# kv with v as loaded as the stationary operand, in four 32-column tiles of TensorE, one head each

## The chip, the cores and the metric

One core of a Trainium2 chip runs the whole program. The metric is the device time of one execution in microseconds (us); lower is better. Engines in the text and in the profile lines: PE is TensorE (its matmuls; PEld is its weight loads), DVE is VectorE, ACT is ScalarE, POOL is GpSimd, SP is SyncE, which issues most DMAs.

## The reference

Two stages, run one after the other: attention with polynomial (sketched) features, then a feed-forward layer (FFN) with squared ReLU.

```python
def phi(x):                                   # r = 8, so 64 features
    a = einsum('rd,bhsd->bhsr', S1, x)
    b = einsum('rd,bhsd->bhsr', S2, x)
    return einsum('bhsi,bhsj->bhsij', a, b).reshape(..., 64)
q_p, k_p = phi(q), phi(k)                     # batch 4, heads 4, seq 1088, head_dim 32
kv  = einsum('bhsf,bhsd->bhfd', k_p, v)
z   = sum(k_p, axis=2)                        # the normaliser
num = einsum('bhsf,bhfd->bhsd', q_p, kv)
den = einsum('bhsf,bhf->bhs', q_p, z)[..., None] + 1e-06
x   = (num / den) as (4352, 128)
out = (relu(x @ w_in) ** 2) @ w_out           # w_in 128x2048, w_out 2048x128
```

## The kernel before

The FFN is a stream of 192 steps (4 batches x 3 chunks of up to 384 rows x 16 column blocks). Each step is one fp16 matmul into `pg`, a ReLU on ACT, a square on ACT or DVE, and one fp32 matmul into `po`. A small planner places the attention of batch n in the steps of the FFN of batch n-1, so that only batch 0's attention stands alone, at the start.

The change touches `kv`. Per batch there are nine row tiles of 128 positions (the last has 64). `kp` holds the 4 x 64 features of a tile. In the kernel before, v is copied into `va`, where each head has 33 columns, 32 of v and one of ones, so that one matmul gives kv and the normaliser. (Of a matmul's two operands, the stationary one is what PEld loads, and the moving one is what the PE record gives as its form, here 128x64.) Rows 64 to 127 of `va`'s last tile are zeroed once, so the short last tile runs on 128 rows too:

```python
# v into va: POOL for batches 1 to 3 (three copies each), ACT and POOL for batch 0
def a_v(b, part, eng, t0=0, n=4):
    ...                                       # [cut] 33 columns per head, column 32 is 1.0

def a_kv(b, t):                               # nine times per batch
    kvp = st[b, "kvp"]
    kp, c0 = st[b, "kp", t]
    for h in range(H):
        c = 64 * (h % 2)                      # two column tiles of 64: heads 0,2 and heads 1,3
        nc.tensor.matmul(
            kvp[c : c + 33, 64 * (h // 2) : 64 * (h // 2) + 64],
            va[b % 2][:, 132 * t + 33 * h : 132 * t + 33 * h + 33],   # stationary, 128 x 33
            kp[:, c0 + 64 * h : c0 + 64 * h + 64],                    # moving, 128 x 64, fp32
            start=(t == 0 and h < 2), stop=(t == NT - 1), skip_group_check=True)

def a_kvz(b):
    kvt = wpool.tile([128, 128], F32, tag="kvt", name="kvt")
    nc.vector.transpose(kvt[:, :], st[b, "kvp"][:, 0:128])
    ...                                       # [cut] eight small copies into the block matrix kvz
    st[b, "kvz"] = kvz                        # read by the nd matmuls: q features x kvz
```

The features of k come from another batch of matmuls (`kf`) which in batches 1 to 3 uses four 32-column tiles already:

```python
for i in range(2):
    for p0 in range(4):
        nc.tensor.matmul(kf[32 * p0 : 32 * p0 + 32, ...], sk[:, 32 * i : 32 * i + 32], kq[...])
```

Of the kernel before, what the change touches and what calls it, by code (L numbers as in the profile page):

```python
# [9 lines left out]
F32 = mybir.dt.float32  # L10
# [3 lines left out]
def _ap(t: bass.AP, p0: int, np_: int, off: int, free):  # L14

    p = list(t.ap)[0]
    return bass.AP(
        t.tensor, t.offset + p0 * p[0] + off, [[p[0], np_]] + [list(d) for d in free]
    )
# [33 lines left out]
def kernel(  # L53
# [11 lines left out]
    nc = tc.nc  # L65

    B, H, S, D = 4, 4, 1088, 32
# [8 lines left out]
    NT = (S + 127) // 128  # L76
    SP = 128 * NT
    TW = [min(128, S - 128 * t) for t in range(NT)]
    E = 2
# [6 lines left out]
    add = mybir.AluOpType.add  # L86
    mult = mybir.AluOpType.mult
# [6 lines left out]
    cpool = ctx.enter_context(tc.tile_pool(name="const", bufs=1))  # L94
    bpool = ctx.enter_context(tc.tile_pool(name="perb", bufs=2))
    wpool = ctx.enter_context(tc.tile_pool(name="work", bufs=2))
    fpool = ctx.enter_context(tc.tile_pool(name="ffn", bufs=5))
    psf = ctx.enter_context(tc.tile_pool(name="psf", bufs=2, space=bass.MemoryType.PSUM))
    psa = ctx.enter_context(tc.tile_pool(name="psa", bufs=1, space=bass.MemoryType.PSUM))
# [30 lines left out]
    kn, qn, vn = {}, {}, {}  # L130
# [52 lines left out]
    kq = cpool.tile([128, SP], F32)  # L183
    nc.gpsimd.memset(_ap(kq, 0, 128, 2 * 32 * NT + 256, [[32 * NT, 2], [1, 32]]), 0.0)
    nc.gpsimd.memset(qT[:, S:SP], 0.0)
    va = []
    for i in range(2):
        t_ = cpool.tile([128, NT * 132], F32, tag=f"va{i}", name=f"va{i}")
        nc.gpsimd.memset(t_[:, (NT - 1) * 132 : NT * 132], 0.0)
        nc.gpsimd.memset(_ap(t_, 0, 128, 32, [[33, NT * H]]), 1.0)  # L190
        va.append(t_)
    kvzs = []
    for i in range(2):
        t_ = cpool.tile([128, E * 132], F32, tag=f"kvz{i}", name=f"kvz{i}")
        nc.gpsimd.memset(t_[:], 0.0)
        kvzs.append(t_)

    st = {}

    def a_kv0(b):  # L200

        st[b, "kvp"] = psa.tile([128, 512], F32, tag="acc", bufs=2, name="kvp")
        nc.vector.memset(st[b, "kvp"][:, 0:128], 0.0)

    a_kv0(0)

    def a_kT(b, part):
        if b > 0 and part < 2:
# [35 lines left out]
    mask_b = [8 + l % 8 for l in range(32)]  # L244
    mask_a = [[4 * e + l // 8 for l in range(32)] for e in range(E)]


    def a_v(b, part, eng, t0=0, n=4):
        a = va[b % 2]
        copy = eng.copy if eng is nc.scalar else eng.tensor_copy  # L250
        if part < 2:
            copy(
                _ap(a, 0, 128, 528 * part + 132 * t0, [[33, H], [132, n], [1, 32]]),
                _ap(vn[b], 0, 128, 512 * part + 32 * t0, [[128, H], [32, n], [1, 32]]),
            )
        else:
            copy(
                _ap(a, 0, 64, 8 * 132, [[33, H], [1, 32]]),
                _ap(vn[b], 0, 64, 1024, [[32, H], [1, 32]]),
            )  # L260

    def a_qT(b, c0, c1):
        nc.vector.transpose(qT[:, c0:c1], qn[b][:, c0:c1])  # L263
# [22 lines left out]
    def a_fs(b, g):  # L286

        n = KG[b][g][1]
        kf = st[b, "kf", g]
        fs = wpool.tile([128, 5 * 64], F32, tag="fs", name="fs")  # L290
        if b == 0:
            for i in range(2):
                nc.scalar.copy(  # L293
                    fs[:, 32 * n * i : 32 * n * i + 32 * n],
                    _ap(kf, 0, 128, 32 * i, [[64, n], [1, 32]]),
                )
        else:
            nc.vector.transpose(fs[:, 0 : 64 * n], kf[:, 0 : 64 * n])
        st[b, "fs", g] = fs

    def a_kp(b, g):
        t0, n = KG[b][g]
        fs = st[b, "fs", g]
        kp = wpool.tile([128, 5 * 256], F32, tag="kp", name="kp", bufs=4)
        nc.vector.tensor_tensor(  # L305
            out=_ap(kp, 0, 128, 0, [[64, 4 * n], [8, 8], [1, 8]]),
            in0=_ap(fs, 0, 128, 0, [[8, 4 * n], [1, 8], [0, 8]]),
            in1=_ap(fs, 0, 128, 32 * n, [[8, 4 * n], [0, 8], [1, 8]]),
            op=mult,
        )  # L310
        for i in range(n):
            st[b, "kp", t0 + i] = kp, 256 * i

    def a_kv(b, t):
        kvp = st[b, "kvp"]
        kp, c0 = st[b, "kp", t]

        for h in range(H):
            c = 64 * (h % 2)
            nc.tensor.matmul(  # L320
                kvp[c : c + 33, 64 * (h // 2) : 64 * (h // 2) + 64],
                va[b % 2][:, 132 * t + 33 * h : 132 * t + 33 * h + 33],
                kp[:, c0 + 64 * h : c0 + 64 * h + 64],
                start=(t == 0 and h < 2),
                stop=(t == NT - 1),
                skip_group_check=True,
            )

    def a_kf2(b):
# [3 lines left out]
    def a_kv9(b):  # L333
        for t in range(NT):
            a_kv(b, t)

    def a_kvz(b):
        kvt = wpool.tile([128, 128], F32, tag="kvt", name="kvt")
        nc.vector.transpose(kvt[:, :], st[b, "kvp"][:, 0:128])
        kvz = kvzs[b % 2]  # L340

        def block(eng, h):
            (eng.copy if eng is nc.scalar else eng.tensor_copy)(
                _ap(kvz, 32 * h, 32, 33 * h, [[132, E], [1, 32]]),
                _ap(kvt, 64 * (h % 2), 32, 64 * (h // 2), [[32, E], [1, 32]]),
            )

        def ones(eng, h):
            (eng.copy if eng is nc.scalar else eng.tensor_copy)(  # L349
                _ap(kvz, 32 * h, 32, 33 * h + 32, [[132, E]]),  # L350
                _ap(kvt, 64 * (h % 2) + 32, 32, 64 * (h // 2), [[32, E]]),
            )


        for h in range(H):
            block(nc.vector if b > 0 or h < 2 else nc.scalar, h)
        for h in range(H):
            ones(nc.gpsimd if b > 0 or h > 1 else nc.vector, h)
        st[b, "kvz"] = kvz

    def a_qc(b, ch, pool=psa, tag="feat"):
# [274 lines left out]
    def replicated(j_, c0, c1, pool, tag):  # L636
        rep[j_, c0] = pool.tile([128, 512], F32, tag=tag, name="rep")
        nc.tensor.matmul(
            rep[j_, c0][:, 0 : c1 - c0], sr[:, 128 * j_ : 128 * j_ + 128], qT[:, c0:c1]
        )  # L640

    def products(c0, c1):
        for e in range(E):
            nc.vector.tensor_tensor(
                out=st[0, "qp", 0, e][:, c0:c1], in0=rep[e, c0][:, 0 : c1 - c0],
                in1=qb[:, c0:c1], op=mult,
            )

    qb = wpool.tile([128, 384], F32, tag="qb", name="qb")
    for e in range(E):  # L650
        st[0, "qp", 0, e] = bpool.tile([128, 384], F32, tag="qp", bufs=4, name="qp")
    replicated(2, 0, 128, psf, "pg")
    a_v(0, 0, nc.scalar)
    a_kp(0, 0)
    a_kp(0, 1)
    for t in range(4):
        a_kv(0, t)
    replicated(0, 0, 128, psa, "feat")
    replicated(1, 0, 128, psa, "tr")
    a_fs(0, 2)  # L660
    a_fs(0, 3)
    a_v(0, 2, nc.gpsimd)
    for h in range(H):
        nc.gpsimd.tensor_copy(
            sq[32 * h : 32 * h + 32, 32 * h : 32 * h + 16], s_T[:, 0:16]
# [2 lines left out]
    make_identity(nc, iden[:])  # L668
    iden16 = cpool.tile([128, 128], F16)
    nc.gpsimd.tensor_copy(iden16[:], iden[:])  # L670
    a_v(0, 1, nc.scalar, 0, 2)
    a_kp(0, 2)
    a_v(0, 1, nc.scalar, 2, 2)
    a_kp(0, 3)
    for t in range(4, 9):
        a_kv(0, t)
    nc.scalar.copy(qb[:, 0:128], rep[2, 0][:, 0:128])
    products(0, 128)

    replicated(2, 128, 384, psf, "pg")  # L680
    replicated(0, 128, 384, psf, "po")
    replicated(1, 128, 384, psf, "po")
    a_kvz(0)
    nc.scalar.copy(qb[:, 128:384], rep[2, 128][:, 0:256])
    products(128, 384)
# [24 lines left out]
    P = _Plan(NS + 4, {"PE": 0.95, "DVE": 1.2, "ACT": 0.6, "POOL": 5.0, "SP": 9.0})  # L710
    for m in range(B * 3 - 1):
        b, ch = divmod(m, 3)
        s0 = 16 * (m + 1)
# [45 lines left out]
    for n in range(1, B):  # L759
        s0 = 48 * (n - 1)  # L760
        P.fix(("ld", n), "SP", 0.0, s0, loads, n)
        for part in range(3):
            P.add(("v", n, part), "POOL", 1.0, [], a_v, n, part, nc.gpsimd, first=s0 + 6)
        for part in range(3):
            P.add(("kT", n, part), "DVE", (0.71, 0.71, 0.2)[part], [], a_kT, n, part, first=s0 + 6)

        need = [("kT", n, part) for part in range(3)] + [("qa", n - 1, 2, 1)]
        P.add(("kf", n), "PE", 1.2, need, a_kf2, n)
        for g in range(2):
            P.add(("fs", n, g), "DVE", 0.4, [("kf", n)], a_fs, n, g)  # L770
            P.add(("kp", n, g), "DVE", 1.15 + 0.3 * g, [("fs", n, g)], a_kp, n, g)
        P.add(("qT", n), "DVE", 1.25, [], a_qT, n, 0, S, first=P.at["kT", n, 2] + 1)
        P.add(("kv0", n), "DVE", 0.15, [("kp", n, 0), ("x3", n - 1, 1)], a_kv0, n)
        need = [("kp", n, 0), ("kp", n, 1), ("kv0", n)] + [("v", n, part) for part in range(3)]
        P.add(("kv", n), "PE", 2.2, need, a_kv9, n)
        q_tasks(n, (0,), 0)
        P.add(("kvz", n), "DVE", 0.9, [("kv", n)], a_kvz, n)
        nd_tasks(n, (0,))
        for ch in (1, 2):
            q_tasks(n, (ch,), 0)  # L780
            nd_tasks(n, (ch,))
# [59 lines left out]
```

## Time and profile before

| | before |
|---|---|
| median time | 203.81 us (203.60 to 204.49, 4 runs) |
| span of the profiled execution | 202.5 us |
| PE / DVE / ACT / POOL busy | 96% / 71% / 71% / 29% |
| kv batch on PE, batches 1 to 3, each | 2.23 us |
| first FFN matmul starts at | 17.42 us |

Lines of the page of the kernel before: busy time of each engine, and the chain of work that ended last as shares by engine and by line.

```profile
span 202.5 us, 3743 instructions
## 1 busy us (share of the span) xinstructions
PE 194.5 (96%) x1209; PEld 127.0 (63%) x1209; DVE 143.0 (71%) x388; ACT 144.1 (71%) x325; POOL 58.2 (29%) x249
...
## 4 chain that ended last, share of the span: by engine, by line
PE 87%; DMA 6%; ACT 2%; SPq 1%; issue 1%; DVE 0%; ACTq 0%
```

PE is the bound: 87% of the chain is PE, the other engines almost nothing. So a microsecond taken off PE's stream between the first and the last FFN matmul is worth a microsecond, and one taken off POOL is worth nothing.

The chain in order of time around batch 1's kv, kernel before (columns: start, length, what):

```profile
40.06 0.65 PE po L513 x2
40.71 2.13 PE kvp L320 x72
42.84 0.27 PE pg L490
```

The 36 fp32 matmuls are 72 records, since an fp32 matmul is two passes. The FFN stream stands still for 2.13 us, three times in the program.

The single records of that batch show what sets its length. These are the times from one record's start to the next, in ns, from the trace; the first number is from the `po` record before:

```
before, kv batch of batch 1 (72 records):
416, 7, 74, 7, 49, 6, 50, 6, 49, 7, 49, 7, 49, 7, ... 49, 7, 152
```

Two records on different column tiles start 7 ns apart, and the pair repeats every 56 ns: a *round*. 36 rounds of 56 ns are 2.02 us. A plain `po` record at 384 columns takes 322 ns, so the 416 ns on entering hold 94 ns that are lost when the tiling changes, and leaving costs about as much again (152 ns in place of 49). I count a kv batch from the end of the `po` record before to the start of the next FFN matmul: 2.554 - 0.322 = 2.23 us.

The start of the program, chain of the kernel before:

```profile
8.00 8.13 DMA w_in_100<-in_moe_w_in_dram
16.15 1.04 ACT w_in L687
17.20 0.45 ACT xT L471 x2
17.69 0.28 PE pg L490
```

### The profile page before, as it was taken

How to read it: one execution, taken by the hardware profiler on the slowest of the kernel's cores; microseconds unless marked ns; L12 is line 12 of the kernel's file. 1: busy time of each engine (PE TensorE's matmuls, PEld its weight loads, DVE VectorE, ACT ScalarE, POOL GpSimd, SP SyncE). 2: the span in 40 equal slices, each digit the busy share in tenths (PEclk: the TensorE clock that was granted, in tenths of full speed). 3: DMA queues.
4: the chain of work that ended last, by engine and by line, in shares of the span. 5: the costliest groups of instructions: out<-in, count | busy, mean ns of one | idle time of the engine just before them, and what ended most of it. 6: DMA issues, size and time to landing. Idle time of an engine off the chain costs nothing.

```text
span 202.5 us, 3743 instructions
## 1 busy us (share of the span) xinstructions
PE 194.5 (96%) x1209; PEld 127.0 (63%) x1209; DVE 143.0 (71%) x388; ACT 144.1 (71%) x325; POOL 58.2 (29%) x249
## 2 busy tenths in 40 slices
PE   7997999999999999999999999999999999999990
PEld 2873675577667555667576655768576655556990
DVE  3975976876497677977757788766847767666750
ACT  3637988857796877686887777686888765766740
POOL 4826447010525830012826500011825300000000
PEclk9999999999999999999999999999999999999999
DMA  6699421110011662020105640020102020110201
GB/s 184 198 263 258 129 72 23 19 23 0 19 31 27 183 169 35 3 39 5 37 13 105 176 132 0 3 41 0 39 12 51 0 32 0 19 23 0 39 0 32
DMA packets 31356, 12.32 MB, mean 61 GB/s; under 512 B 23338, under 2 KB 29930, under 8 KB 31338
## 3 DMA queue, kind: packets, MB, share of 16 engines
q1 hardware_dynamic: 30886, 12.00, 24.3%
q8 instruction: 9, 0.15, 0.3%
q10 hardware_dynamic: 452, 0.10, 0.3%
q14 instruction: 9, 0.07, 0.1%
HBM read 8.78 MB, written 2.23 MB: 54 GB/s over the span
## 4 chain that ended last, share of the span: by engine, by line
PE 87%; DMA 6%; ACT 2%; SPq 1%; issue 1%; DVE 0%; ACTq 0%
PE po L513 55%; PE pg L490 15%; PE nd L389 7%; DMA w_in_100<-in_moe_w_in_dram 4%; PE kvp L320 3%; PE qc L363 3%; DMA vn<-in_v_dram 2%; PE pt L530 2%; PE kf L279 2%; ACT gt L499 2%; SPq L104 1%; ACT w_in L687 1%; SPq L114 0%; ACT xT L471 0%; SPq L160 0%
## 5 line engine op out<-in xcount | busy, mean ns | idle before, releaser
L499 ACT ACTIVATE gt<-pg 128x384 f32<-128x384 f32 (+2 forms) x193 | 89.0, 464 | 38.5 <-PE pg L490 37.6
L490 PE MATMUL pg<-xT,w_in 128*128 128x384 f16 (+2 forms) x193 | 61.1, 316 | 1.1 <-ACT xT L471 0.7
L545 POOL COPY br<-beta 32x3 f32<-32x3 f32 x192 | 42.6, 222 | 50.1 <-DVE beta L453 42.5
L490 PEld LDWEIGHTS <-w_in 128*128 128x128 f16 x193 | 18.9, 98 | 19.6 <-issue 1.9
L373 DVE STREAM_SHUFFLE qa<-qc 128x384 f32<-128x384 f32 x22 | 12.0, 592 | 0.1
L389 PEld LDWEIGHTS nd<-kvz_127,qp 128*128 128x128 f32 x72 | 10.0, 190 | 3.0 <-DVE qp L378 0.2
L553 DVE STREAM_TRANSPOSE oT<-po 128x384 f32<-128x384 f32 (+1 forms) x11 | 6.2, 564 | 7.9 <-PE po L513 7.9
L378 DVE TENSOR_TENSOR qp<-qa,qb 128x384 f32<-128x384 f32 x22 | 11.7, 567 | 0.1
L389 PEld LDWEIGHTS nd<-kvz_125,qp 128*128 128x128 f32 x72 | 9.9, 190 | 2.7 <-issue 0.2
L305 DVE TENSOR_TENSOR kp<-fs 128x512 f32<-128x512 f32 (+3 forms) x10 | 10.8, 1108 | 0.5 <-ACT fs L293 0.4
L389 PE MATMUL nd<-kvz_127,qp 128*128 128x132 f32 x72 | 10.3, 277 | 0.0
L389 PE MATMUL nd<-kvz_125,qp 128*128 128x132 f32 x72 | 10.2, 280 | 0.0
L349 POOL COPY kvz_127<-kvt 32x2 f32<-32x2 f32 x8 | 1.5, 185 | 26.3 <-PE pg L490 16.9
L363 PE MATMUL qc<-qT,sq 128*128 128x384 f32 x22 | 8.8, 491 | 0.0
L446 DVE TENSOR_TENSOR xs<-nd,sc 128x384 f16<-128x384 f32 (+2 forms) x13 | 6.7, 522 | 0.3
L263 DVE STREAM_TRANSPOSE qT<-qn 128x1088 f32<-128x1088 f32 (+2 forms) x5 | 5.3, 1061 | 2.3 <-DMA qn<-in_q_dram 2.3
L368 DVE STREAM_SHUFFLE qb<-qc 128x384 f32<-128x384 f32 x11 | 6.5, 588 | 0.0
L559 DVE TENSOR_TENSOR ob<-oT,br 128x384 f32<-128x384 f32 (+1 forms) x11 | 6.3, 572 | 0.0
L405 DVE TENSOR_SCALAR den<-nd 128x12 f32<-128x12 f32 x12 | 2.0, 170 | 5.8 <-PE nd L389 5.8
L410 DVE TENSOR_REDUCE mx<-nd 128x12 f32<-128x384 f32 x12 | 5.9, 495 | 0.0
L363 PEld LDWEIGHTS qc<-qT,sq 128*128 128x128 f32 x22 | 4.1, 190 | 2.7
L621 PE MATMUL warm<-zero 128*128 128x512 f16 x13 | 4.6, 516 | 1.2 <-DVE zero L143 1.2
(711 smaller groups left out, 414.2 us busy)
## 6 DMA issues: line engine op xcount, KB each, us to landing
vn<-in_v_dram SPq DMA_DIRECT2D x32, 64.0 KB, 2.8
kn<-in_k_dram SPq DMA_DIRECT2D x3, 544.0 KB, 8.1
qn<-in_q_dram SPq DMA_DIRECT2D x3, 544.0 KB, 3.5
out_dram<-ob SPq DMA_DIRECT2D x32, 48.0 KB, 1.8
w_in_100<-in_moe_w_in_dram SPq DMA_DIRECT2D x2, 512.0 KB
w_o<-in_moe_w_out_dram SPq DMA_DIRECT2D x2, 512.0 KB, 11.4
out_dram<-ob SPq DMA_DIRECT2D x12, 40.0 KB, 1.8
qn<-in_q_dram SPq DMA_DIRECT2D x1, 352.0 KB
```

Source lines behind the costliest of these rows:

```text
L305: nc.vector.tensor_tensor(out=_ap(kp, 0, 128, 0, [[64, 4 * n], [8, 8], [1, 8]]), in0=_ap(fs, 0, 128, 0, [[8, 4 * n], [1, 8], [0, 8]]), in1 ...
L363: nc.tensor.matmul(qc[:, 0:384], sq[:, :], qT[:, 384 * ch : 384 * ch + 384])
L368: nc.vector.stream_shuffle(in_=st[b, "qc", ch][:, 0:384], out=qb[:, :], mask=mask_b)
L373: nc.vector.stream_shuffle(in_=st[b, "qc", ch][:, 0:384], out=qa[:, :], mask=mask_a[e])
L378: nc.vector.tensor_tensor(out=qp[:, :], in0=st[b, "qa", ch, e][:, :], in1=st[b, "qb", ch][:, :], op=mult)
L389: nc.tensor.matmul(nd[:, 132 * o : 132 * o + 132], st[b, "qp", ch, e][:, 128 * o : 128 * o + 128], st[b, "kvz"][:, 132 * e : 132 * e + 132 ...
L446: nc.vector.tensor_tensor(out=_ap(st[b, "xs", ch], 0, 128, 128 * o, [[32, 4 * n], [1, 32]]), in0=_ap(st[b, "nd", ch], 0, 128, 132 * o, [[3 ...
L490: nc.tensor.matmul(pg[:, c0:c1], w_in[:, 128 * c : 128 * c + 128], st[b, "xT"][:, 384 * ch + c0 : 384 * ch + c1],)
L499: nc.scalar.activation(gt[:, c0:c1], pg[:, c0:c1], Relu)
L513: nc.tensor.matmul(st["po", b, ch][:, c0:c1], w_o[:, 128 * c : 128 * c + 128], g2s[i][1][:, c0:c1], start=first, stop=(c == NFF - 1), skip ...
L545: nc.gpsimd.tensor_copy(_ap(st[b, "br"], 32 * dm, 32, 12 * ch + p0, [[4, 3]]), st[b, "beta"][32 * p0 : 32 * p0 + 32, 3 * ch : 3 * ch + 3],)
L559: nc.vector.tensor_tensor(out=_ap(ob, 0, 128, 0, [[32, n // 32], [1, 32]]), in0=_ap(st["oT", b, ch], 0, 128, 0, [[32, n // 32], [1, 32]]), ...
```

## The change

The intent is to make kv cheaper on PE and to drop the copies of v. v is used as loaded, 32 columns per head, so that four heads fit in four 32-column tiles. The normaliser then needs matmuls of its own, with a stationary of ones. To keep these few, DVE first adds the features of eight tiles into one (batches 1 to 3); in batch 0 this is not done, and it pays 36 extra matmuls. The block matrix is made by one masked product in place of eight copies.

```diff
     def a_kv(b, t):
-        kvp = st[b, "kvp"]
+        if t == 0:
+            st[b, "kvp"] = psa.tile([128, 512], F32, tag="acc", bufs=2, name="kvp")
         kp, c0 = st[b, "kp", t]
+        n, v0, dv = (128, 512 * (t // 4) + 32 * (t % 4), 128) if t < 8 else (64, 1024, 32)
         for h in range(H):
-            c = 64 * (h % 2)
             nc.tensor.matmul(
-                kvp[c : c + 33, 64 * (h // 2) : 64 * (h // 2) + 64],
-                va[b % 2][:, 132 * t + 33 * h : 132 * t + 33 * h + 33],
-                kp[:, c0 + 64 * h : c0 + 64 * h + 64],
-                start=(t == 0 and h < 2),
+                st[b, "kvp"][32 * h : 32 * h + 32, 0:64],
+                _ap(vn[b], 0, n, v0 + dv * h, [[1, 32]]),
+                kp[0:n, c0 + 64 * h : c0 + 64 * h + 64],
+                start=(t == 0),
...
+    def a_z(b, kp, c0, last):                 # four matmuls, stationary ones[128, 32]
...
+    def a_ks1(b):                             # DVE: 128x1024 add; a_ks2: 512, then 256
...
     def a_kv9(b):
         for t in range(NT):
             a_kv(b, t)
+        a_z(b, *st[b, "kp", 8], False)
+        a_z(b, st[b, "ks"], 0, True)
...
     def a_kvz(b):
-        ...                                   # eight copies per batch on DVE, ACT and POOL
+        nc.vector.tensor_tensor(              # one masked product, 128 x 264
+            out=_ap(kvz, 0, 128, 0, [[132, E], [33, H], [1, 33]]),
+            in0=_ap(kvt, 0, 128, 0, [[64, E], [0, H], [1, 33]]),
+            in1=_ap(own, 0, 128, 0, [[0, E], [1, H], [0, 33]]), op=mult)
...
-            P.add(("v", n, part), "POOL", 1.0, [], a_v, n, part, nc.gpsimd, first=s0 + 6)
...
-        P.add(("kv", n), "PE", 2.2, need, a_kv9, n)
+        P.add(("ks1", n), "DVE", 1.15, [("kp", n, 1)], a_ks1, n)
+        P.add(("ks2", n), "DVE", 1.0, [("ks1", n)], a_ks2, n)
+        P.add(("kv", n), "PE", 1.4, [("ks2", n), ("x3", n - 1, 1)], a_kv9, n)
```

Cut: the memsets of `va`, `kvp` and `kvz`, the calls of `a_v`, and batch 0's calls of `a_z` after each `a_kv`.

More of the change, by code (lines that the diff above doesn't have):

```diff
@@ L185 @@
     nc.gpsimd.memset(qT[:, S:SP], 0.0)
-    va = []
-    for i in range(2):
-        t_ = cpool.tile([128, NT * 132], F32, tag=f"va{i}", name=f"va{i}")
-        nc.gpsimd.memset(t_[:, (NT - 1) * 132 : NT * 132], 0.0)
-        nc.gpsimd.memset(_ap(t_, 0, 128, 32, [[33, NT * H]]), 1.0)
-        va.append(t_)
     kvzs = []
     for i in range(2):
-        t_ = cpool.tile([128, E * 132], F32, tag=f"kvz{i}", name=f"kvz{i}")
-        nc.gpsimd.memset(t_[:], 0.0)
-        kvzs.append(t_)
+        kvzs.append(cpool.tile([128, E * 132], F32, tag=f"kvz{i}", name=f"kvz{i}"))
+    own = cpool.tile([128, H], F32)
+    nc.gpsimd.memset(own[:], 0.0)
+    for h in range(H):
+        nc.gpsimd.memset(own[32 * h : 32 * h + 32, h : h + 1], 1.0)
+    ones = cpool.tile([128, 32], F32)
+    nc.gpsimd.memset(ones[:], 1.0)
     st = {}
-    def a_kv0(b):
-        st[b, "kvp"] = psa.tile([128, 512], F32, tag="acc", bufs=2, name="kvp")
-        nc.vector.memset(st[b, "kvp"][:, 0:128], 0.0)
-    a_kv0(0)
     def a_kT(b, part):
@@ L245 @@
     mask_a = [[4 * e + l // 8 for l in range(32)] for e in range(E)]
-    def a_v(b, part, eng, t0=0, n=4):
-        a = va[b % 2]
-        copy = eng.copy if eng is nc.scalar else eng.tensor_copy
-        if part < 2:
-            copy(
-                _ap(a, 0, 128, 528 * part + 132 * t0, [[33, H], [132, n], [1, 32]]),
-                _ap(vn[b], 0, 128, 512 * part + 32 * t0, [[128, H], [32, n], [1, 32]]),
-            )
-        else:
-            copy(
-                _ap(a, 0, 64, 8 * 132, [[33, H], [1, 32]]),
-                _ap(vn[b], 0, 64, 1024, [[32, H], [1, 32]]),
-            )
     def a_qT(b, c0, c1):
@@ L314, in a_kv, with a_ks2 @@
     def a_kv(b, t):
-        kvp = st[b, "kvp"]
+        if t == 0:
+            st[b, "kvp"] = psa.tile([128, 512], F32, tag="acc", bufs=2, name="kvp")
         kp, c0 = st[b, "kp", t]
+        n, v0, dv = (128, 512 * (t // 4) + 32 * (t % 4), 128) if t < 8 else (64, 1024, 32)
         for h in range(H):
-            c = 64 * (h % 2)
             nc.tensor.matmul(
-                kvp[c : c + 33, 64 * (h // 2) : 64 * (h // 2) + 64],
-                va[b % 2][:, 132 * t + 33 * h : 132 * t + 33 * h + 33],
-                kp[:, c0 + 64 * h : c0 + 64 * h + 64],
-                start=(t == 0 and h < 2),
+                st[b, "kvp"][32 * h : 32 * h + 32, 0:64],
+                _ap(vn[b], 0, n, v0 + dv * h, [[1, 32]]),
+                kp[0:n, c0 + 64 * h : c0 + 64 * h + 64],
+                start=(t == 0),
                 stop=(t == NT - 1),
                 skip_group_check=True,
+            )
+    def a_z(b, kp, c0, last):
+        for h in range(H):
+            nc.tensor.matmul(
+                st[b, "kvp"][32 * h : 32 * h + 32, 64:128],
+                ones[:, :],
+                kp[:, c0 + 64 * h : c0 + 64 * h + 64],
+                start=False,
+                stop=last,
+                skip_group_check=True,
+            )
+    def a_ks1(b):
+        ks = st[b, "ks"] = wpool.tile([128, 1024], F32, tag="ks", bufs=1, name="ks")
+        nc.vector.tensor_tensor(
+            out=ks[:, :], in0=st[b, "kp", 0][0][:, 0:1024], in1=st[b, "kp", 4][0][:, 0:1024],
+            op=add,
+        )
+    def a_ks2(b):
+        ks = st[b, "ks"]
+        for w in (512, 256):
+            nc.vector.tensor_tensor(
+                out=ks[:, 0:w], in0=ks[:, 0:w], in1=ks[:, w : 2 * w], op=add
             )
@@ L335, in a_kv9 @@
             a_kv(b, t)
+        a_z(b, *st[b, "kp", 8], False)
+        a_z(b, st[b, "ks"], 0, True)
     def a_kvz(b):
         kvt = wpool.tile([128, 128], F32, tag="kvt", name="kvt")
-        nc.vector.transpose(kvt[:, :], st[b, "kvp"][:, 0:128])
+        nc.vector.transpose(
+            _ap(kvt, 0, 128, 0, [[32, 2], [64, E], [1, 32]]),
+            _ap(st[b, "kvp"], 0, 128, 0, [[64, 2], [32, E], [1, 32]]),
+        )
         kvz = kvzs[b % 2]
-        def block(eng, h):
-            (eng.copy if eng is nc.scalar else eng.tensor_copy)(
-                _ap(kvz, 32 * h, 32, 33 * h, [[132, E], [1, 32]]),
-                _ap(kvt, 64 * (h % 2), 32, 64 * (h // 2), [[32, E], [1, 32]]),
-            )
-        def ones(eng, h):
-            (eng.copy if eng is nc.scalar else eng.tensor_copy)(
-                _ap(kvz, 32 * h, 32, 33 * h + 32, [[132, E]]),
-                _ap(kvt, 64 * (h % 2) + 32, 32, 64 * (h // 2), [[32, E]]),
-            )
-        for h in range(H):
-            block(nc.vector if b > 0 or h < 2 else nc.scalar, h)
-        for h in range(H):
-            ones(nc.gpsimd if b > 0 or h > 1 else nc.vector, h)
+        nc.vector.tensor_tensor(
+            out=_ap(kvz, 0, 128, 0, [[132, E], [33, H], [1, 33]]),
+            in0=_ap(kvt, 0, 128, 0, [[64, E], [0, H], [1, 33]]),
+            in1=_ap(own, 0, 128, 0, [[0, E], [1, H], [0, 33]]),
+            op=mult,
+        )
         st[b, "kvz"] = kvz
@@ L652 @@
     replicated(2, 0, 128, psf, "pg")
-    a_v(0, 0, nc.scalar)
     a_kp(0, 0)
@@ L657 @@
         a_kv(0, t)
+        a_z(0, *st[0, "kp", t], False)
     replicated(0, 0, 128, psa, "feat")
@@ L661 @@
     a_fs(0, 3)
-    a_v(0, 2, nc.gpsimd)
     for h in range(H):
@@ L670 @@
     nc.gpsimd.tensor_copy(iden16[:], iden[:])
-    a_v(0, 1, nc.scalar, 0, 2)
     a_kp(0, 2)
-    a_v(0, 1, nc.scalar, 2, 2)
     a_kp(0, 3)
@@ L676 @@
         a_kv(0, t)
+        a_z(0, *st[0, "kp", t], t == 8)
     nc.scalar.copy(qb[:, 0:128], rep[2, 0][:, 0:128])
@@ L762 @@
         for part in range(3):
-            P.add(("v", n, part), "POOL", 1.0, [], a_v, n, part, nc.gpsimd, first=s0 + 6)
-        for part in range(3):
             P.add(("kT", n, part), "DVE", (0.71, 0.71, 0.2)[part], [], a_kT, n, part, first=s0 + 6)
@@ L772 @@
         P.add(("qT", n), "DVE", 1.25, [], a_qT, n, 0, S, first=P.at["kT", n, 2] + 1)
-        P.add(("kv0", n), "DVE", 0.15, [("kp", n, 0), ("x3", n - 1, 1)], a_kv0, n)
-        need = [("kp", n, 0), ("kp", n, 1), ("kv0", n)] + [("v", n, part) for part in range(3)]
-        P.add(("kv", n), "PE", 2.2, need, a_kv9, n)
+        P.add(("ks1", n), "DVE", 1.15, [("kp", n, 1)], a_ks1, n)
+        P.add(("ks2", n), "DVE", 1.0, [("ks1", n)], a_ks2, n)
+        P.add(("kv", n), "PE", 1.4, [("ks2", n), ("x3", n - 1, 1)], a_kv9, n)
         q_tasks(n, (0,), 0)
```

## The prediction

> **What bounds the kernel now.** TensorE. In the busy table PE has 96% of the 202.5 us span, DVE 71%, ACT 71%, POOL 29%; in busy time by stretches PE is never idle from 20 to 185 us; in the chain of waits PE holds 87%. Before about 17.4 us the chain runs through the landing of w_in's second half (8.13 us, to 16.13 us), its cast on ACT (1.04 us) and the xT copies behind it; batch 0's kv is not on it.
>
> Single matmul records show why PE is full: an fp32 matmul is two records, 322 ns each at 384 columns. Records on different column tiles overlap. In the kv batch (33-column stationary, two 64-column tiles) two records start 7 ns apart and the pair repeats every 56 ns: 72 records, 2.13 us in the chain, three times (batches 1 to 3). In the kf batch (four 32-column tiles) four records start 7 ns apart and repeat every 109 ns at 128 columns. So four tiles run at once, as the Trainium skill, "TensorEngine Tiling (Array Packing)", section "Key Properties", says; it also says that a change of mode drains the array, and the trace agrees: about 95 ns entering and again leaving each such batch.
>
> **What changes.** PE, batches 1 to 3: 36 kv matmuls plus 8 for the normaliser, 88 records in fours: 22 rounds x 56 ns = 1.23 us instead of 36 x 56 = 2.02 us. The last kv tile has 64 rows; if that is another mode, two more drains (0.19 us). Saving 0.6 to 0.78 us each, 1.8 to 2.35 us in all, on the critical path.
> Batch 0: 72 matmuls in fours, again 36 rounds. The va copies (ACT 0.63 and 0.72 us, POOL 0.28) go, kvz comes perhaps 0.5 us earlier; that stage waits for w_in, so I count nothing.
> DVE, each of batches 1 to 3: added ks1 (about 1.2 us, as the 128x1024 kp product), ks2 (estimate 0.9), masked product (estimate 0.4); removed the 0.17 us memset and four copies of 0.19. Net about +1.6 us. The instruction order shows kv one or two FFN steps (0.81 us each) later, and about two squares per batch moved from DVE to ACT. Both have room: over 34 to 48 us DVE is busy 10.9 of 14.0 us, ACT 10.3. POOL's lost copies are off the path.
>
> **Critical part.** About -2.0 us on PE; up to 0.3 us may come back in short waits where DVE and ACT are fullest.
>
> **Prediction: 201.9 us, range 200.9 to 204.6. Faster by over 2%: 3%; within 2%: 95%; slower by over 2%: 2%.**
>
> **What would show each step.** Right: kvp batches of 88 records in 1.3 to 1.5 us, starts 7 ns apart in fours, period 56 ns; PE without idle from 20 to 185 us; first FFN matmul still near 17.4 us; DVE busy up about 4 to 5 us, ACT about 2. Wrong: a kvp batch of 2.4 us; PE waiting for ks, kvp or qp; ACT late with gt.
>
> **What would make it wrong.** (1) PE may not feed instructions so fast. Both column-tiled batches of before average 27 to 28 ns per record, and the Trainium skill, "TensorE: Matmul & The Clock Gate", Part 1, gives a start-to-start floor of about 25 ns; no stream in this trace beats that for longer than bursts of four. If it binds, 88 records take 2.4 us and the kernel loses about 1 us: 204.9. One chance in five. (2) The longer DVE chain kp, ks1, ks2 makes PE wait in batch 1, where kp ends just as kv starts. (3) The w_in landing moves.

## The result, and the profile after

| | before | after |
|---|---|---|
| median time | 203.81 us (4 runs) | 202.40 us (202.35 to 202.47, 4 runs) |
| ratio | | 0.9925, 95% interval 0.9902 to 0.9949 |
| span of the profiled execution | 202.5 us | 200.7 us |
| kv batch, batches 1 to 3, each | 2.23 us | 1.73 us |
| first FFN matmul starts at | 17.42 us | 16.93 us |
| first FFN matmul to last matmul | 179.67 us | 178.40 us |

A ratio here is the mean time of one kernel's runs over that of the other's of the same rounds, so it is not quite the ratio of the medians that are quoted. The interval says that it is faster, by 0.5 to 1.0%.

The same lines of the page, kernel after:

```profile
span 200.7 us, 3928 instructions
## 1 busy us (share of the span) xinstructions
PE 193.1 (96%) x1329; PEld 125.1 (62%) x1329; DVE 143.7 (72%) x375; ACT 144.7 (72%) x326; POOL 50.4 (25%) x225
...
## 4 chain that ended last, share of the span: by engine, by line
PE 84%; DMA 6%; DVE 3%; ACT 2%; SPq 1%; issue 1%; ACTq 0%
```

PE is still the bound. But DVE, absent from the chain before, now has 3% of it (about 6 us), although its busy time hardly moved.

The chain around batch 1's kv, kernel after:

```profile
41.19 0.65 PE po L512 x2
41.84 1.28 PE kvp L299 x72
43.12 0.36 PE kvp L310 x16
43.48 0.27 PE pg L489
```

1.28 + 0.36 = 1.64 us where there were 2.13. The starts of its 88 records, ns after the record before:

```
after, kv batch of batch 1 (88 records), one round to a line:
416, 6, 7, 7            first round, after po
60, 6, 7, 7
35, 7, 7, 6             a plain round is 55 to 56 in all; 14 of these in a row
...
149, 7, 7, 6            the 64-row tail of kv, first pass
60, 7, 7, 6             its second pass
146, 7, 7, 6            first normaliser round, 128 rows again
60, 7, 7, 6
36, 7, 6, 6 / 37, 7, 6, 7, then 152 to the next FFN matmul
```

Four records now share a round of 56 ns. This confirms the first half of the calculation: 22 rounds x 56 ns = 1.23 us. It also shows what was under-counted. On entering and again on leaving the 64-row tile, the gaps are 149 + 60 and 146 + 60 ns where plain rounds have 36 + 36: 113 + 24 + 110 + 24 = 271 ns per batch. The kernel before has no such gaps: all its kv records have 128 rows, since the tail of `va` was padded with zeros. Dropping the copies brought the 64-row tail in.

DVE's 3% sits in one place, from 54.8 to 60.7 us, where batch 1's third chunk is prepared. Part of the chain there, kernel after:

```profile
57.02 0.57 DVE qa L372
...
59.12 0.41 DVE qp L377
59.52 0.59 DVE qa L372
60.11 0.02 issue
60.13 0.58 DVE qp L377
60.72 0.04 issue
60.76 0.94 PE nd L388 x6
```

From 56 to 62 us the chain of the kernel before is PE all through. From the gaps between PE records in excess of the matmul's own length (those of over 50 ns in excess), PE waits 0.44 us there before and 0.66 us after; with the smaller gaps it is 0.46 and 0.66. PE's busy time does not show this well (5.99 of 6.00 us before, 5.89 after): a matmul record that waits for the next one is drawn as busy.

The body of the program can now be added up: three kv batches at 2.232 - 1.733 = 0.50 us each save 1.50 us, the waits near 60 us give 0.22 back, which leaves 1.28; measured from the first FFN matmul to the last matmul, the program is 179.67 - 178.40 = 1.27 us shorter. The rest of the span's 1.8 us is the start, and that needs the experiments: is 17.42 to 16.93 us an effect of the change or chance?

The start in the profile of the kernel after:

```profile
7.94 7.71 DMA w_in_100<-in_moe_w_in_dram
15.64 0.02 issue
15.67 1.04 ACT w_in L684
16.71 0.50 ACT xT L470 x2
```

It is the same path as before, with w_in landing half a microsecond sooner.

### The profile page after: what moved, and what is told of

It is laid out like the page before. It is cut to its first block, busy times and chain, and to the rows that moved or that the text cites. A ratio compares the mean times of both kernels' runs of the same rounds, so it can differ in the third digit from the quotient of the medians.

```text
span 200.7 us, 3928 instructions
## 1 busy us (share of the span) xinstructions
PE 193.1 (96%) x1329; PEld 125.1 (62%) x1329; DVE 143.7 (72%) x375; ACT 144.7 (72%) x326; POOL 50.4 (25%) x225
## 3 DMA queue, kind: packets, MB, share of 16 engines
HBM read 8.78 MB, written 2.23 MB: 55 GB/s over the span
## 4 chain that ended last, share of the span: by engine, by line
PE 84%; DMA 6%; DVE 3%; ACT 2%; SPq 1%; issue 1%; ACTq 0%
PE po L512 54%; PE pg L489 14%; PE nd L388 7%; DMA w_in_100<-in_moe_w_in_dram 4%; PE qc L362 3%; DMA vn<-in_v_dram 2%; PE kvp L299 2%; PE pt L529 2%; PE kf L256 2%; ACT gt L498 1%; SPq L104 1%; DVE qa L372 1%; PE kvp L310 1%; ACT w_in L684 1%; DVE qp L377 0%
## 5 line engine op out<-in xcount | busy, mean ns | idle before, releaser
L544 POOL COPY br<-beta 32x3 f32<-32x3 f32 x192 | 43.5, 227 | 104.4 <-DVE beta L452 97.1
L377 DVE TENSOR_TENSOR qp<-qa,qb 128x384 f32<-128x384 f32 x22 | 11.2, 544 | 0.0
L299 PE MATMUL kvp<-kp,vn 128*32 128x64 f32 (+1 forms) x288 | 6.3, 222 | 0.0
L299 PEld LDWEIGHTS kvp<-kp,vn 128*32 128x32 f32 (+1 forms) x288 | 4.9, 109 | 2.2 <-DVE ks L322 0.5
L558 DVE TENSOR_TENSOR ob<-oT,br 128x384 f32<-128x384 f32 (+1 forms) x11 | 5.8, 530 | 0.0
```

What stands on the lines that cost most here:

```text
L299: nc.tensor.matmul(st[b, "kvp"][32 * h : 32 * h + 32, 0:64], _ap(vn[b], 0, n, v0 + dv * h, [[1, 32]]), kp[0:n, c0 + 64 * h : c0 + 64 * h + ...
L377: nc.vector.tensor_tensor(out=qp[:, :], in0=st[b, "qa", ch, e][:, :], in1=st[b, "qb", ch][:, :], op=mult)
L544: nc.gpsimd.tensor_copy(_ap(st[b, "br"], 32 * dm, 32, 12 * ch + p0, [[4, 3]]), st[b, "beta"][32 * p0 : 32 * p0 + 32, 3 * ch : 3 * ch + 3],)
```

## The experiments

The theory (A): the gain is PE time of the kv batches, set by the number of rounds and of mode changes. Rivals: (B) the removed copies or the shorter start make the gain; (C) the added DVE work decides; and smaller ones stated at each run.

### Control: the changed kernel again (`after_again`)

No edit.

> The changed kernel once more, as the control of this group and for a second profile of its start. Theory A (the gain is TensorE time in the kv batches of batches 1 to 3: 36 rounds of 56 ns became 22, less the mode switches of the 64-row tail): each kv batch again 1.73 us from the end of the matmul before to the next one, against 2.23 in the kernel before, so -1.50 us; ratio to the kernel before 0.992 to 0.994. Theory B (a good part of the gain is the start: first FFN matmul at 16.93 instead of 17.42 us): the first FFN matmul stays near 16.9 us in every profile of a kernel without v copies. If it is chance of the loads, it scatters between 16.9 and 17.4 us from profile to profile, whatever the kernel.

Measured: 202.98 us against 204.09, ratio 0.9933 (0.9912 to 0.9954); kv batches 1.73 us; first FFN matmul at 17.44 us. So the gain repeats, and the early start of the first profile does not. What the start waited for is another path this time. Its chain:

```profile
1.22 4.45 PE warm L620 x10
5.67 2.48 PE kf L247 x18
...
16.51 0.63 DVE xs L445 x2
17.14 0.05 issue
17.19 0.30 PE xp L461 x2
17.49 0.02 issue
17.51 0.38 ACT xT L470
17.89 0.04 issue
17.93 0.28 PE pg L489
```

This chain runs through batch 0's own attention from PE's warm-up matmuls on, and w_in is not on it. The reason is in the records of the ten warm-up matmuls: one starts every 427 ns until PE's clock is released and every 216 ns after. The release came at 3.96 us in the first profile of this kernel and at 6.53 us here, so that all the warm-up and the first five `kf` records ran slowly.

### Control: the kernel before again (`before_again`)

No edit; one look only.

> The kernel before once more, for a second profile of its start. kv batches 2.23 us each from the end of the matmul before to the next one. If the start is the later of two paths, the landing of w_in and batch 0's own chain from the release of the TensorE clock on, both of which scatter from run to run, then the first FFN matmul lies between 16.4 and 17.6 us whatever the kernel, and batch 0's chain (first kp to first transpose of xs) takes 9.9 us as in the first profile of this kernel.

Measured: 204.38 us (one run, state unknown), kv batches 2.23 us, clock released at 6.60 us, batch 0's chain 9.89 us, first FFN matmul at 17.33 us. Its chain at the start runs through batch 0 as well, not through w_in. Over the profiles:

| profile | clock released, us | batch 0: first kp to first transpose of xs, us | second cast of w_in starts, us | first FFN matmul, us | first FFN to last matmul, us |
|---|---|---|---|---|---|
| before | 4.24 | 9.90 | 16.15 | 17.42 | 179.67 |
| before_again | 6.60 | 9.89 | 14.95 | 17.33 | 179.81 |
| after | 3.96 | 9.87 | 15.67 | 16.93 | 178.40 |
| after_again | 6.53 | 9.96 | 15.22 | 17.44 | 178.55 |
| copies_kept | 5.58 | 10.51 | 15.52 | 17.59 | 178.53 |
| blocks_copied | 5.18 | 10.06 | 14.76 | 17.04 | 178.54 |
| tail_rows_128 | 5.29 | 9.60 | 13.95 | 16.52 | 177.72 |
| tail128_again | 4.30 | 9.59 | 14.48 | 16.46 | 177.71 |

Two paths race at the start, and both scatter from run to run for reasons outside this change. The body, the last column, repeats to 0.15 us.

### The tail on 128 rows (`tail_rows_128`)

```diff
-        vn[b] = bpool.tile([128, 1024 + 128], F32, tag="vn", name="vn")
+        vn[b] = vns[b % 2]                     # two fixed tiles, rows 64 to 127 of the tail zeroed once
...
-  else (64, 1024, 32)
+  else (128, 1024, 32)
```

> The last kv tile runs on 128 rows (64 of them zero, set once), nothing else changed. Theory A: the tail costs two extra changes of tiling mode, 137 ns each by the gaps in the records (149 and 60 ns, 146 and 60 ns, where a round has 36 and 7). Without them each kv batch takes 1.46 us instead of 1.73, the kernel is 0.8 us faster than the changed kernel, ratio to the kernel before 0.988 to 0.990. Rival: the gaps are the wait for the tail's loads or for ks, not the mode: then the gaps stay and the time is that of the changed kernel.

Measured: 201.61 us against 204.09, ratio 0.9870 (0.9849 to 0.9891). The batch in PE's timeline of this kernel (start, length, what):

```profile
41.49 1.21 PE L304 MATMUL kvp<-kp,vn 128*32 128x64 f32 x72
42.52 0.29 PE L315 MATMUL kvp<-kp,ones 128*32 128x64 f32 x8
42.63 0.30 PE L315 MATMUL kvp<-ks,ones 128*32 128x64 f32 x8
```

The gaps inside are gone (every round from the third on is 55 to 57 ns), and a kv batch takes 1.46 us. The loads and the sums are the same as before, so the rival is refuted: the 271 ns were the two mode changes. (The two fixed tiles of v are not the cause: `tail128_batch0` below has them too, with a 64-row tail in batches 1 to 3, and its kv batches take 1.73 us.) The body is 0.83 us shorter than that of `after_again`, as expected; the ratio moved a little more than expected, which the run on batch 0 below takes up.

### The tail last (`tail_last`)

```diff
-        for t in range(NT):
+        for t in range(NT - 1):
             a_kv(b, t)
         a_z(b, *st[b, "kp", 8], False)
         a_z(b, st[b, "ks"], 0, True)
+        a_kv(b, NT - 1)
```

> The 64-row tail of kv goes to the end of the batch, after the normaliser, for batches 1 to 3. Theory A (cost per change of mode): one change fewer, since the batch leaves column tiling there anyway: 0.137 us less per batch, 1.60 us instead of 1.73, 0.4 us off the changed kernel in all. Rival (64-row matmuls are slow in themselves): no change in the sum, 1.73 us.

Measured: 202.43 us against 204.09, ratio 0.9908 (0.9887 to 0.9929). The batch in PE's timeline:

```profile
42.40 1.10 PE L299 MATMUL kvp<-kp,vn 128*32 128x64 f32 x64
43.32 0.29 PE L310 MATMUL kvp<-kp,ones 128*32 128x64 f32 x8
43.43 0.29 PE L310 MATMUL kvp<-ks,ones 128*32 128x64 f32 x8
43.66 0.32 PE L299 MATMUL kvp<-kp,vn 64*32 64x64 f32 x8
```

A kv batch takes 1.60 us, 0.136 less than in the changed kernel: with the same eight 64-row records, but one change of mode fewer; the body is 178.11 us. By the ratios alone this would not be settled, since their intervals overlap. So the cost belongs to the change of mode and not to 64-row matmuls. The form column, `64*32` against `128*32`, is where the mode can be read.

### The copies of v kept (`copies_kept`)

```diff
-                _ap(vn[b], 0, n, v0 + dv * h, [[1, 32]]),
+                _ap(va[b % 2], 0, n, 132 * t + 33 * h, [[1, 32]]),
```
with `va`, its memsets and all copies of the kernel before put back.

> The changed kernel, but kv reads v from the copies that the kernel before made (on POOL, in batch 0 on ACT), so that only the copies' removal is undone. Theory A: the copies are off the critical path; time within 0.3 us of the changed kernel, kv batches 1.73 us. Theory B (the copies' removal is what pays, by an earlier start or a freer POOL and DVE): time goes back towards the kernel before, by 0.5 us or more, and the first FFN matmul back to about 17.4 us.

Measured: 202.87 us against 204.09, ratio 0.9935 (0.9910 to 0.9961), that of the control; kv batches 1.73 us; body 178.53 us as in the control. Removing the copies does nothing for the body. In batch 0 the chain is longer in this profile (10.51 us against 9.96): it runs through the landing of the second part of v, at 9.61 us, and a copy on ACT behind it. That is one late landing and not a steady cost of the copies, for the kernel before has them too and 9.90 and 9.89 us. In the time nothing of it is seen beyond the scatter of the start, so of rival B nothing is shown.

### The masked product undone (`blocks_copied`)

```diff
-        nc.vector.tensor_tensor(out=..., in0=..., in1=own..., op=mult)
+        for h in range(H):
+            (nc.vector.tensor_copy if b > 0 or h < 2 else nc.scalar.copy)(
+                _ap(kvz, 32 * h, 32, 33 * h, [[132, E], [1, 33]]),
+                _ap(kvt, 32 * h, 32, 0, [[64, E], [1, 33]]))
```

> The changed kernel with the masked product undone: the block matrix is filled by four copies per batch of 32 rows (DVE; in batch 0 two on DVE and two on ACT) into buffers zeroed once. Theory A: this part of the change moves nothing by itself; DVE about 0.3 us more per batch, kv batches 1.73 us, the time within 0.3 us of the changed kernel, ratio to the kernel before 0.992 to 0.996. Rival (one instruction instead of eight shortens the way from kv to the next matmuls): slower than the changed kernel by 0.5 us or more.

Measured: 202.89 us against 204.43, ratio 0.9925 (0.9907 to 0.9943); kv batches 1.73 us; body 178.54 us. This part of the change moves nothing in the body; batch 0's chain is 10.06 us here against 9.87 and 9.96, within what one profile can tell.

### The sums on PE (`sums_on_pe`)

```diff
-        a_z(b, *st[b, "kp", 8], False)
-        a_z(b, st[b, "ks"], 0, True)
+        for t in range(NT):
+            a_z(b, *st[b, "kp", t], t == NT - 1)
...
-        P.add(("ks1", n), "DVE", 1.15, ...)     # and ks2
```

> The changed kernel without the sums on DVE: the normaliser is 36 more matmuls in each of batches 1 to 3, as batch 0 has it, and DVE is relieved of about 2 us per batch. Theory A (TensorE time decides): 14 rounds of 56 ns more per batch than the changed kernel, kv batch 2.51 us instead of 1.73, +2.3 us, less up to 0.6 us of waits on DVE near 58 to 61 us that go; ratio to the kernel before 1.002 to 1.007, so the change without its DVE sums would be a loss. Rival (the 1.6 us of added DVE work per batch eats the gain): faster than the changed kernel.

Measured: 205.14 us against 203.89, ratio 1.0047 (1.0024 to 1.0070); kv batches 2.52 us; PE's waits near 60 us fell to 0.45 us, as in the kernel before. With the normaliser on PE, the 72 matmuls in fours are 36 rounds, as many as in the kernel before, and the 0.28 us per batch over its 2.23 are the two changes of mode of the tail. So the four tiles alone would have been a loss; it is the sums on DVE that make the change pay. Rival C has its small share: the added DVE work costs 0.2 us of waits, and no more. (That the kv batch is longer here is not why the waits fell: `head_by_head`, next, keeps the sums on DVE, has a still longer batch, and waits 0.66 us.)

### Head by head (`head_by_head`)

On the kernel with the 128-row tail, batches 1 to 3:

```diff
-        for t in range(NT):
-            a_kv(b, t)
+        for h in range(H):
+            for t in range(NT):
+                a_kv(b, t, (h,))
```

> The kernel with the 128-row tail, but in batches 1 to 3 kv goes head after head, nine matmuls in the same 32-column tile after each other, instead of four tiles in turn; the same matmuls, the same number. Theory A (the gain is overlap of records in different tiles): each of the 72 kv records takes its own 56 ns, 4.0 us instead of 1.0, kv batch 4.5 us instead of 1.46, +9 us in all, ratio to the kernel before about 1.03. Rival (fewer columns to load, or reads of v in place, are what is cheaper): no change from the kernel with the 128-row tail.

Measured: 208.85 us against 203.89, ratio 1.0241 (1.0212 to 1.0270). In PE's timeline the group of kv records that took 1.21 us for 72 records in the kernel with the 128-row tail is now (three of the 72 stand apart, among the normaliser's):

```profile
41.50 3.46 PE L304 MATMUL kvp<-kp,vn 128*32 128x64 f32 x69
```

The same matmuls in another order: records on one tile start 56 ns apart, and the kv batch takes 3.88 us in place of 1.46. I had expected 4.5; the trace shows that the records at a change of head and the normaliser's records still start beside others, which saves the difference. So the change's gain is the overlap of tiles, and it depends on issuing the heads in turn.

### The last tile into the sums too (`tail128_fold`)

On the kernel with the 128-row tail, four matmuls fewer per batch and one 128x256 add more on DVE:

```diff
+        nc.vector.tensor_tensor(out=ks[:, 0:256], in0=ks[:, 0:256], in1=kp[:, c0 : c0 + 256], op=add)
...
-        a_z(b, *st[b, "kp", 8], False)
```

> The kernel with the 128-row tail, and the last tile's features added to the sums on DVE too, so that four matmuls (two rounds) per batch go and DVE has about 0.35 us more. Theory A: kv batch 1.35 us instead of 1.46, 0.33 us in all, less what the waits near 58 to 61 us grow by (DVE is on the chain there), so 0 to 0.3 us faster than the kernel with the 128-row tail; ratio to the kernel before 0.985 to 0.988.

Measured: 201.65 us against 203.89, ratio 0.9888 (0.9862 to 0.9915): no gain over the 128-row tail. In batches 2 and 3 kv takes 1.35 us as expected, but in batch 1 1.71, since PE waits for the sum:

```profile
41.91 1.21 PE L304 MATMUL kvp<-kp,vn 128*32 128x64 f32 x72
43.27 0.32 PE L315 MATMUL kvp<-ks,ones 128*32 128x64 f32 x8 [0.15 <-DVE ks L339]
```

In the changed kernel the last sum starts at 42.19 us, takes 0.43 us, and is read at 43.18 us, with 0.56 us to spare; the shorter batch and the longer sum use this up. What two rounds save in three batches (0.33 us) is lost in one wait of 0.36.

### The 128-row tail again (`tail128_again`)

No edit to the kernel of `tail_rows_128`.

> The kernel with the 128-row tail once more, as the control of this group. Ratio to the kernel before 0.985 to 0.990, kv batches 1.46 us, batch 0's chain (first kp to first transpose of xs) 9.6 us as in its first profile.

Measured: 201.37 us against 204.43, ratio 0.9849 (0.9831 to 0.9867); kv batches 1.46 us; batch 0's chain 9.59 us.

### The 128-row tail in batch 0 only (`tail128_batch0`)

```diff
+        n = 128 if b == 0 else n
```
with the two fixed tiles of v as in `tail_rows_128`.

> The changed kernel with the 128-row tail in batch 0 only. The full 128-row tail gained 1.3 us over the changed kernel by the ratios, of which batches 1 to 3 explain 0.81. Theory A: batch 0's own chain is often the later of the two paths that the start waits for (in several profiles the loads of w_in land well before), and the two mode changes in it cost 0.27 us: chain 9.6 us instead of 9.9 to 10.0, time 0.2 to 0.3 us below the changed kernel, kv batches of 1 to 3 still 1.73. Rival: the start waits for w_in, as I predicted; no change, and the rest of the gain was chance or the fixed buffers of v.

Measured: 202.37 us against 204.43, ratio 0.9902 (0.9883 to 0.9920); batch 0's chain 9.62 us; body 178.53 us, as in the changed kernel. The chain is shorter by 0.25 to 0.34 us, and the first FFN matmul came at 16.70 us. The ratio is 0.2 to 0.3% below those of the changed kernel, in the direction of the theory, though the intervals overlap: the shorter chain is shown by the trace, its worth in time is not settled.

### Another order on DVE (`tail128_qfirst`)

On the kernel with the 128-row tail, in batch 1 the features of q for the third chunk come ahead of the second chunk's scaling:

```diff
+        q_tasks(n, (1,), 0)
+        if n == 1:
+            q_tasks(n, (2,), 0)
+        nd_tasks(n, (1,))
...
```

> The kernel with the 128-row tail, and in batch 1 the features of q for the third chunk are put ahead of the scaling of the second on DVE. Near 58 to 61 us PE waits 0.66 us in all, and the chain of waits there runs through DVE for some 5 us. Theory (DVE's order, loaded by the sums, makes the last nd of batch 1 wait for qp): nd no longer waits for qp (0.38 us gone), 0.2 to 0.4 us faster than the kernel with the 128-row tail, ratio to the kernel before 0.984 to 0.987. Rival (ACT, with relu and square in every step there, holds PE as well): the wait only moves to the FFN matmuls, and the time stays.

Measured: 200.81 us against 204.43, ratio 0.9839 (0.9816 to 0.9862). The chain near 60 us is PE alone again:

```profile
56.85 0.54 PE po L517 x2
57.39 1.12 PE nd L393 x8
58.51 0.14 PE pg L494
```

PE's waits there fell from 0.66 to 0.18 us (0.23 with the smaller gaps), and the body is 177.16 us against 177.71 for its control. Of these 0.55 us some 0.13 are not this edit's: PE's gaps in the first microseconds of the FFN add up to 1.14 us here and 1.27 in the control, and the same two values come from two profiles of one kernel (`after` and `after_again`). This is the fastest kernel. That it beats the kernel before is clear; that it beats the 128-row tail is shown by the body of the trace, while the intervals of the two ratios overlap.

## Why the prediction was right or wrong

I predicted 201.9 us, with a range of 200.9 to 204.6 and 95% for "within 2%"; measured were 202.40 us. The mechanism held; one term was mis-sized and one reason was wrong.

- *PE is the bound, and only rounds on PE count.* Right. The chain is 87% PE before and 84% after; putting back the copies or the small block copies left the body of the program within 0.02 us of the control.
- *22 rounds of 56 ns.* Right: four records 5 to 8 ns apart, 55 to 57 ns a round. The Trainium skill, "TensorEngine Tiling (Array Packing)", section "Key Properties", says that tiles operate independently, and head_by_head shows what this is worth: 2.42 us per batch.
- *"if that is another mode, two more drains (0.19 us). Saving 0.6 to 0.78 us each, 1.8 to 2.35 us in all".* This is the term that was off. It is another mode, and the two changes cost 0.27 us per batch: each loses 110 to 113 ns, where I had counted the 95 ns that I had read off the trace on entering a batch, and delays the second round by another 24 ns. The saving is 0.50 us each and 1.50 in all. Moving the tail to the end takes off one change (0.136 us), giving it 128 rows takes off both.
- *"up to 0.3 us may come back in short waits".* Right in size, 0.22 us, and nearly in place: over 56 to 62 us DVE was busy 91% of the time in the kernel before, though over 20 to 26 us it was fuller, 99%. The added sums are the cause: without them the wait is 0.45 us, with them 0.66.
- *PE may not feed instructions so fast.* It did not bind. The floor of about 25 ns between starts, which the Trainium skill gives in "TensorE: Matmul & The Clock Gate", Part 1, is not a floor across tiles: the records here start every 14 ns on average in plain rounds, every 17 ns over a whole batch with the two changes of mode.
- *"batch 0's kv is not on it" and "that stage waits for w_in, so I count nothing".* The count of nothing was about right: batch 0's chain was 9.90 us before and 9.87 to 9.96 after. The reason was wrong, being read from one execution. In the second profile of the kernel before, batch 0 is on the chain and w_in is not. That nothing came of it is luck: with the 64-row tail taken out of batch 0, its chain is 9.57 to 9.62 us (`tail128_batch0` and the other kernels with the 128-row tail), so the rest of the change shortens it by about 0.3 us, and the tail's two changes of mode, which I had not counted there, lengthen it by as much.
- *DVE busy up 4 to 5 us, ACT about 2.* Wrong: 0.7 and 0.6. I had named the squares that the planner moves from DVE to ACT but not subtracted them: DVE's squares fell from 88 to 82, 46.3 to 43.0 us, and ACT's rose from 105 to 111, 53.5 to 56.5 us, while ACT lost its copies. No run shows that this mattered for the time.

The sum: -1.50 us of kv, +0.22 of waits, and the start unchanged within its scatter give about -1.3 us; measured are -1.41 by the medians and -0.75% (about -1.5 us) by the ratio.

Open: what sets the moment of the clock's release and of w_in's landing. Together they moved the first FFN matmul of one and the same kernel from 16.93 to 17.44 us, and no experiment here touched them.

## What to carry to other kernels

Count small matmuls in rounds, one round being as long as one matmul on one tile, and issue the tiles in turn: the same matmuls, tile after tile, took 3.88 us in place of 1.46. Then count the changes of mode, rows as well as columns: padding one 64-row tail with zeros, as the dropped copies had done by the way, took another 0.83 us off the body, where the whole change had taken 1.27. And do not judge a start that waits for the later of two paths from one profile.

## What the Trainium skill lacked or had wrong

- "TensorEngine Tiling (Array Packing)", section "Key Properties", says that a change of mode drains the array but gives no cost. Here a change between 128 and 64 rows within 32-column tiling costs 0.136 us (two of them 0.271 us per batch), of which 24 ns are a late second round after it. What the rest of the time goes into, no run shows.
- "TensorE: Matmul & The Clock Gate", Part 1, gives a floor of about 25 ns between the starts of small matmuls. Across four column tiles the starts here are about 7 ns apart in a round and 14 ns on average over the 88 records of a batch of `tail_rows_128`; Part 1 does not say that its floor does not hold across tiles, though the starts of concurrent tiles in Part 3 imply it.
- The same page, Part 3, puts concurrent tiles about 4 ns apart; here, in fp32 on column tiles, it is 5 to 8 ns, mostly 6 or 7.
- The same page, Part 1, puts the release of the clock at about 4 us of matmuls, give or take 0.5 us, though it adds that the number of slow matmuls differs from run to run. The matmuls here start at 1.22 us and the release came between 3.96 and 6.62 us over 14 profiles, so 2.7 to 5.4 us after the first matmul: a wider spread. Batch 0's first kp moves with it by up to 0.6 us (6.24 to 6.86 us in the kernel before).
